# Q of two heads and two token tiles as seven block products in place of eight, in the second half of an attention kernel

## The chip, the cores and the metric

The kernel runs on one core of a Trainium2 chip. The metric is the device time of one execution in microseconds (us). The kernel before takes 1949.78 us (median of three runs, 1949.32 to 1949.82).

## The reference

```python
x = A_x                                   # 1 x 2048 x 640
xn = _layernorm(x, axis=-1)
# A: 32 heads of 128; of the cache only the last W = 512 keys are used
q = (xn @ wq)                             # 640 -> 32 x 128
scores = einsum(q, k) * 128 ** -0.5       # 2048 x 512 for each head
p = softmax(scores)
s = einsum(p, v) -> reshape(2048, 4096) @ wo   # back to 640
# B: dense block on the same xn
h = relu(xn @ w1 + b1) ** 2               # 640 -> 1728
g = silu(h @ w2 + b2)                     # 1728 -> 640
out = x + s * g
```

All arrays are float32.

## The kernel before, in words

Everything is held transposed: features on the 128 partitions, tokens along the free axis. The 2048 tokens are four tiles of 512 (0 to 3); the 640 features are five chunks of 128. Each operand of a matmul is split into two parts, `hi` (a copy by ACT, ScalarE, that rounds) and `lo` (what is left, by a subtraction on DVE, VectorE, or on POOL, GpSimd), and each product is three passes, hi x hi, hi x lo and lo x hi (`triple`). A pass is one matmul instruction with its weight load, 128x128 weights by 512 columns.

First come layernorm and the dense block for tiles 0 to 2 (its result g goes to DRAM as `g_d`; the normalised tiles, split, go there as `xT_d`). In that part tiles 1 and 2 (`T1`, `T2`) already get their 640 -> 1728 product by Winograd's form of Strassen's scheme: four blocks by four blocks in seven products (`t_sums`, `w_sums`, `prod`).

Then comes attention, in two halves: the first takes tiles 0 and 1, the second tiles 2 and 3. A half goes through 16 groups of two heads; a group has four units, one for each pair of a tile and a head. In a unit i, PE (TensorE) makes the scores `s` (four banks of PSUM, 12 matmuls), Q of a unit two later (`pq`, 5 chunks x 3 passes = 15 matmuls), `o` of the unit before (12), and the output products `r` of an earlier pair (15 on average; the sums over heads are kept in `acc`). That is 54 matmuls.

DVE takes the maxima of the four score banks (tile `rdm`), ACT gathers them (three small copies), DVE makes a row of them (`rowm`), which goes through DRAM by SP's queue (SyncE) and comes back broadcast as `bm`; DVE subtracts it from the scores (`e<-s,bm`, four times; this frees the score banks for the next unit). ACT takes the exponential and the hi part, POOL the lo part (`pt`) and the sum (`su`), DVE folds the sums (`rds`), gathered by ACT in the same way, and makes a reciprocal row (`sq`, `rows`), which comes back as `bs` and scales `o` on DVE. ACT and DVE then split `o` into `ot`. Q is split by ACT (`q_hi`) and DVE (`q_lo`). DVE also adds each `r` to `acc`.

What every engine does in which order is a plan: `at(when, f, ...)` puts a call at a time, the list is sorted by time, and every engine runs its own instructions in that order. The planner's times are only ranks; each instruction then waits for its data and for the buffers that it writes. PE's stream of instructions is also padded: `align(i, slot)` (L1411) calls `addr_align(BLOCK, ...)` with BLOCK = 256 before each of the four score products of a unit and once behind them, which puts no-operations (NOP) in until the next instruction's place is `FIRST_SLOT + 128 i + slot` modulo 256. `SLOTS` is (0, 11, 22, 33, 42). A unit thus has 128 places, and 86 of them lie between the last slot of one unit and the first of the next. A matmul takes two places, its weight load and itself.

In the second half tile 0's and 1's results are finished: the sums, x and g come from DRAM (`load_finish`), DVE multiplies (`fs<-fs,fg`), POOL adds, and SP stores; ten such pieces, one every four units. After the last units comes the dense block for tile 3 (`late_up`, tile `lu`; `late_down`, tile `ly`), which begins already in units 126 and 127, where no Q is left to make.

Of the kernel before, what the change touches and what calls it, by code (L numbers as in the profile page):

```python
# [14 lines left out]
P = 128  # L15
# [10 lines left out]
def kernel(  # L26
# [64 lines left out]
    s_d = [dpool.tile([P, DC, NT], F32, name=f"s_d{t}") for t in range(NTILE // 2)]  # L91
    h_d = {f: dpool.tile([P, NT], F32, name=f"h_d{f}") for f in range(FC - 4, FC)}
# [7 lines left out]
    T1, T2 = 1, 2  # L100
# [461 lines left out]
    def t_sums(q):  # L562
        e, o = 2 * q, 2 * q + 1
# [29 lines left out]
    def w_sums(p):  # L593
        a, b = WR[p, 0], WR[p, 1]
        a11, a12, a21, a22 = (w[:, k : 2 * NQ2 : 2, :] for w in (a, b) for k in range(2))
# [21 lines left out]
    def w_split(p, k):  # L617
# [10 lines left out]
        else:  # L628
            hi, lo = WB[p, "a2"] = wb("a2", [P, NQ2, P], f"wc{p}")
            pieces = [(hi, lo, b[:, 1 : 2 * NQ2 : 2, :])]  # L630
# [6 lines left out]
    def left(p, what, q):  # L637
        kind, at_ = {
            "a11": ("a1", (2 * q,)),
            "a12": ("a1", (2 * q + 1,)),  # L640
# [8 lines left out]
    def right(what, q):  # L649
        if what[0] == "t":  # L650
            return [w[:, q, :] for w in TS[int(what[1]) - 1]]
        k, j = int(what[1]) - 1, int(what[2])
        return [w[:, 2 * q + k, :] for w in XS[(T1, T2)[j - 1]]]
# [195 lines left out]
    def bank(name, k):  # L849
        return pools["psa"].tile([P, NT], F32, tag=f"qr{k}", name=name, bufs=1)  # L850
# [10 lines left out]

    def load_xT(hf, t, i, cs, queue=sp):
        queue.dma_start(raw(XT[hf, t][i])[:, cs, :], xT_d[hf * TPH + t][i][:, cs, :])

    def raw_tile(kind, name):
        n = D if kind in "qo" else W
        pool_of = pools["ep"] if kind in "qk" else ap
        return pool_of.tile([P, n], F32, tag=f"raw{kind}", name=name, bufs=1)
# [14 lines left out]

    def prep(kind, hf, h, eng=None):
        shape = {"q": [P, DC, DH], "k": [P, W], "v": [P, KC, DH], "o": [P, D]}[kind]
        home = {"q": WQ, "k": KT, "v": VV, "o": WO}[kind]
        hi, lo = home[hf, h] = pair(f"w{kind}", shape, f"w{kind}{hf}_{h}", 2 * G if kind == "o" else G)
        src = RAW.pop((kind, hf, h))
        act.activation(hi, src, AF.Copy)
        (eng or pool).tensor_tensor(lo, src, raw(hi), op=ALU.subtract)  # L890

    def q_mm(i, cs):
# [4 lines left out]
        for c in cs:  # L897
            triple(
                QPS[i],
                (ws[0][:, c, :], ws[1][:, c, :]),  # L900
# [3 lines left out]
            )  # L904

# [36 lines left out]
    def row(i, what):  # L942
# [13 lines left out]
        for args in BEHIND.pop((i, what), ()):  # L956
            load_xT(*args)
        bc = ap.tile([P, NT], F32, tag=f"b{what}", name=f"b{what}{i}", bufs=2)
# [12 lines left out]
    def p_hi(i, k):  # L971
        PT[i, k] = [
            ap.tile([P, 2, NT], F32R, tag=f"pt{n}", name=f"pt{i}_{k}_{n}", bufs=3)
# [21 lines left out]
    def v_mm(i, c):  # L995
        hf, g, t, h = units[i]
        if c == 0:
            if i % 2 or i < UPG:
# [53 lines left out]
    def load_finish(n, hf, t, d):  # L1052
        t0 = (hf * TPH + t) * NT
# [6 lines left out]
                "g": g_d[hf * TPH + t][:, d, :],  # L1060
# [7 lines left out]
    def finish(hf, t, d):  # L1068
        a = ACC[hf, t][:, d, :] if hf else FX.pop(("s", hf, t, d))
        (dve if hf else pool).tensor_tensor(a, a, FX.pop(("x", hf, t, d)), op=ALU.add)  # L1070
# [556 lines left out]
```

## Time and profile before

| | |
|---|---|
| median of three runs | 1949.78 us |
| span of the profiled execution | 1947.7 us, first to last instruction |
| PE, busy in the span | 1941.0 us, 8585 matmuls |
| DVE | 1599.4 us |
| ACT | 1242.3 us |
| POOL | 1348.4 us |
| DMA | 246.43 MB, mean 127 GB/s |
| units of attention | 128, from about 289 us on; the second half from about 1072 us on |

How to read it: busy time of an engine is the union of its instructions' times. In the timeline, a row merges equal neighbours of one engine: start, time from first start to last end, what, how many; brackets hold the idle time before it and what ended that. PE's matmuls overlap, so the distance of two starts is what counts there. The profiled execution is given by its span; what lies around the span is not listed for it, and the median of the runs stands 2.1 us above the span.

### The profile page before, as it was taken

The numbers are of one execution on the slowest core, as the hardware profiler recorded it, in microseconds if no ns is written. First come the engines' busy times: TensorE is split into PE (matmuls) and PEld (weight loads), VectorE is DVE, ScalarE is ACT, GpSimd is POOL, SyncE is SP. The second block draws the span as 40 slices with busy tenths as digits, with TensorE's granted clock in tenths as the row PEclk, the third lists the DMA queues.
The fourth block names the chain that finished last, engine by engine and source line by source line (L and its number), as shares of the span: only waits on it lengthen the run. The fifth ranks groups of instructions, "written<-read, shape, count | busy, mean of one in ns | idle before, by whom it ended". The sixth has DMA issues, their size and how long they took to land.

```text
span 1947.7 us, 28638 instructions
## 1 busy us (share of the span) xinstructions
PE 1941.0 (100%) x8585; PEld 1606.9 (83%) x8585; DVE 1599.4 (82%) x2760; ACT 1242.3 (64%) x2152; POOL 1348.4 (69%) x732
## 2 busy tenths in 40 slices
PE   9999999999999999999999999999999999999999
PEld 8888888888888888888888888888888888888887
DVE  6864747788888888888888878888888888888865
ACT  5665536766666666666666676666666666666643
POOL 1022107888888888888888878888888888888841
PEclk9999999999999999999999999999999999999999
DMA  6657953332222222222235433333333333323253
GB/s 207 198 195 252 367 190 114 95 93 91 91 90 92 93 91 91 92 92 92 92 100 183 140 109 109 114 114 114 114 114 114 113 115 113 98 92 92 84 189 119
DMA packets 147783, 246.43 MB, mean 127 GB/s; under 512 B 25188, under 2 KB 47478, under 8 KB 146358
## 3 DMA queue, kind: packets, MB, share of 16 engines
q1 hardware_dynamic: 144918, 232.65, 37.8%
q0 software_dynamic: 2576, 11.80, 1.5%
q8 instruction: 77, 1.26, 0.2%
q14 instruction: 68, 0.56, 0.1%
q10 hardware_dynamic: 144, 0.16, 0.0%
HBM read 213.59 MB, written 30.95 MB: 126 GB/s over the span
## 4 chain that ended last, share of the span: by engine, by line
PE 99%; DMA 0%; POOL 0%; DVE 0%; issue 0%; ACT 0%; SPq 0%; POOLq 0%
PE r L77 22%; PE pq L77 22%; PE o L77 18%; PE s L77 18%; PE py L77 7%; PE ph L77 3%; PE ly L77 2%; PE wa L77 2%; PE lu L77 2%; PE wy L77 1%; PE wx L77 1%; PE eu L77 1%; DMA xb<-in_x_dram 0%; PE px L77 0%; POOL xb L77 0%; DVE st L77 0%
## 5 line engine op out<-in xcount | busy, mean ns | idle before, releaser
L77 POOL TENSOR_TENSOR pt<-e,pt 128x1024 fp32r<-128x1024 f32 x256 | 614.8, 2402 | 113.3 <-ACT pt L77 62.3
L77 PE MATMUL r<-ot,wo 128*128 128x512 f32 x1920 | 496.6, 389 | 0.0
L77 PE MATMUL pq<-ax,wq 128*128 128x512 f32 x1920 | 456.0, 389 | 0.0
L77 PEld LDWEIGHTS r<-ot,wo 128*128 128x128 f32 x1920 | 360.4, 188 | 74.9
L77 PEld LDWEIGHTS pq<-ax,wq 128*128 128x128 f32 x1920 | 360.4, 188 | 74.8
L77 PE MATMUL o<-pt,wv 128*128 128x512 f32 x1536 | 369.2, 389 | 0.0
L77 PE MATMUL s<-q,wk 128*128 128x512 f32 x1536 | 369.0, 389 | 0.0
L77 DVE TRANSPOSE_TENSOR_REDUCE rdm<-s 128x16 f32<-128x512 f32 x512 | 348.3, 713 | 8.0 <-PE s L77 8.0
L77 ACT ACTIVATE e<-e 128x1024 f32<-128x1024 f32 x256 | 269.6, 1053 | 121.4 <-DVE e L77 74.3
L77 PEld LDWEIGHTS o<-pt,wv 128*128 128x128 f32 x1536 | 288.2, 188 | 60.2 <-POOL pt L77 0.4
L77 PEld LDWEIGHTS s<-q,wk 128*128 128x128 f32 x1536 | 288.3, 188 | 59.9
L77 DVE TENSOR_TENSOR e<-s,bm 128x512 f32<-128x512 f32 x512 | 311.9, 664 | 4.5 <-DMA bm<-m_d 4.1
L77 POOL TENSOR_TENSOR su<-e,e 128x1024 f32<-128x1024 f32 x128 | 308.7, 2412 | 0.0
L77 ACT ACTIVATE pt<-e 128x1024 fp32r<-128x1024 f32 x256 | 272.0, 1062 | 6.9
L77 ACT ACTIVATE rdm<-rdm 32x64 f32<-32x64 f32 x384 | 97.7, 254 | 184.6 <-DVE rdm L77 181.5
L77 DVE TENSOR_TENSOR acc<-r,acc 128x512 f32<-128x512 f32 x300 | 203.5, 678 | 13.2 <-PE r L77 13.1
L77 DVE TENSOR_TENSOR ot<-o,ot 128x512 fp32r<-128x512 f32 x128 | 88.5, 691 | 86.0 <-ACT ot L77 86.0
L77 DVE TRANSPOSE_TENSOR_REDUCE rds<-su 128x32 f32<-128x1024 f32 x128 | 158.3, 1236 | 0.2 <-POOL su L77 0.2
L77 ACT ACTIVATE q<-pq 128x512 fp32r<-128x512 f32 x128 | 76.6, 598 | 117.8 <-PE pq L77 117.8
L77 ACT ACTIVATE rds<-rds 32x32 f32<-32x32 f32 x384 | 89.5, 233 | 62.3 <-DVE rds L77 58.9
L77 POOL TENSOR_TENSOR wo<-or,wo 128x640 fp32r<-128x640 f32 x64 | 101.1, 1579 | 31.6 <-ACT wo L77 31.6
L77 POOL TENSOR_TENSOR wv<-vr,wv 128x512 fp32r<-128x512 f32 x64 | 83.2, 1300 | 54.1 <-ACT wv L77 54.1
(172 smaller groups left out, 2008.3 us busy)
## 6 DMA issues: line engine op xcount, KB each, us to landing
bm<-m_d SPq DMA_DIRECT2D x128, 256.0 KB
bs<-s_d SPq DMA_DIRECT2D x128, 256.0 KB
qr<-in_wq_dram SPq DMA_DIRECT2D x64, 320.0 KB
or<-in_wo_dram SPq DMA_DIRECT2D x64, 320.0 KB
kr<-in_kT_dram SPq DMA_DIRECT2D x64, 256.0 KB
vr<-in_v_dram SPq DMA_DIRECT2D x64, 256.0 KB
cw<-in_w_dram SPq DMA_DIRECT2D x26, 320.0 KB
h_m<-r SPq DMA_DIRECT2D x26, 256.0 KB
```

The source lines that it names most:

```text
L77: ins = method(*args, **kwargs)
```

## The change

The halves of attention take other tiles: the first tiles 0 and 3, the second tiles 1 and 2, for which the first part of the kernel already has the sums `T1` to `T4` of blocks of x. These go to DRAM (`TS_d`) by eight DMAs of POOL's queue. The blocks are now halves of the features (chunks 0, 1 and chunks 2, 3) and no longer the even and the odd chunks; the fifth chunk is done apart (`q_rest`).

In the first half, each group's two `wq` of the later use are turned into the sums S1 to S4 on DVE (`q_sums`, four additions of 128x256), split by ACT and POOL (`q_sum_hi`, `q_sum_lo`) and stored to DRAM with the plain blocks (`q_store`, nine calls a group). In the second half no `wq` is loaded or split; the ready pieces come from DRAM (`q_piece`, four a group) and the T blocks through a ring of three buffers (`q_ring`, six calls a group).

A group's Q in the second half is then, over the four units that begin two units ahead of it (slots 0 to 3):

- slot 0: product 5 in bank b, kept by ACT (`q_keep`, tile `qp5`); product 1 in bank a, copied by ACT to bank b (`q_seed`);
- slot 1: product 2 and a rest into b (Q of the first unit); product 6 into a; DVE adds `qp5` to a and puts it in b (`q_add`);
- slot 2: product 7 into a, kept by ACT (`qu3`); a rest and product 4 into a (Q of the second unit); DVE adds `qp5` to `qu3` and puts it in a (`q_add`);
- slot 3: product 3 and a rest into b (third unit); a rest into a (fourth unit).

The two banks that Q now holds were shared with `r` before. In the second half `r` has one bank (`psx`, tag x) and `o` has one. To make room, the buffers of `e` and `pt` go from three to two, that of `bs` from two to one. The times of `r` change with them (`R_AT_Q`), also in the last units. Only tile 0's five pieces are finished in the second half; tiles 1 and 2 are finished at the end (ten pieces), tile 3 in the late gate, for which its sums (`late_sum`) and its x tile (`load_late_x`) are loaded back.

How DVE's order moves, in unit 80 and the end of unit 79 (second half): the last maximum of unit 79 up to the first score to be shifted. Before:

```order
L77 TENSOR_REDUCE rdm79_13625<-s79_3_13636 128x16
L77 TENSOR_TENSOR acc1_1_12385<-r75_2_13551,acc1_1_12385 128x512
L77 TENSOR_REDUCE rowm79_13659<-rdm79_13625 32x16
L77 TENSOR_TENSOR o77_13578<-o77_13578,bs77_13576 128x512
L77 TENSOR_TENSOR ot77_13672<-o77_13578,ot77_13672 128x512
L77 TENSOR_REDUCE rds78_13681<-su78_13651 128x2x16
L77 SCALAR_TENSOR_TENSOR q81_1_13685<-pq81_13647,q81_0_13684 128x512
L77 TENSOR_TENSOR acc1_1_12385<-r75_4_13687,acc1_1_12385 128x512
L77 TENSOR_REDUCE sq2_2910<-rds78_13681 32x16
L77 RECIPROCAL sq2_2910<-sq2_2910 32x16
L77 STREAM_TRANSPOSE rows78_13707<-sq2_2910 32x32
L77 TENSOR_TENSOR e79_0_13729<-s79_0_13612,bm79_13663 128x512
```

The same place after:

```order
L77 TENSOR_REDUCE rdm79_14080<-s79_3_14091 128x16
L77 TENSOR_REDUCE rowm79_14119<-rdm79_14080 32x16
L77 TENSOR_TENSOR acc1_1_12867<-r75_3_14097,acc1_1_12867 128x512
L77 TENSOR_TENSOR o77_14031<-o77_14031,bs77_14029 128x512
L77 TENSOR_TENSOR ot77_14129<-o77_14031,ot77_14129 128x512
L77 TENSOR_REDUCE rds78_14141<-su78_14105 128x2x16
L77 SCALAR_TENSOR_TENSOR q80_1_14145<-pq20b_14006,q80_0_14144 128x512
L77 TENSOR_TENSOR pq20b_14166<-pq20a_13994,qp520_14001 128x512
L77 TENSOR_REDUCE sq2_2984<-rds78_14141 32x16
L77 RECIPROCAL sq2_2984<-sq2_2984 32x16
L77 STREAM_TRANSPOSE rows78_14172<-sq2_2984 32x32
L77 TENSOR_TENSOR acc1_1_12867<-r75_4_14151,acc1_1_12867 128x512
```

An `acc` that stood between the last maximum and the row made of the maxima now stands behind the row; the addition `pq20b` is new, and an `acc` stands ahead of the shift.

How ACT's order moves in unit 80 (slot 2 of group 20), from the gather of the maxima on. Before:

```order
L77 ACTIVATE rdm80_13763<-rdm80_13763 32x16x4 x3
L77 ACTIVATE pt79_1_0_13793<-e79_1_13735 128x1024
L77 ACTIVATE ot78_13808<-o78_13715 128x512
L77 ACTIVATE q82_0_13830<-pq82_13804 128x512
L77 ACTIVATE rds79_13817<-rds79_13817 32x16x2 x3
```

After:

```order
L77 ACTIVATE rdm80_14221<-rdm80_14221 32x16x4 x3
L77 ACTIVATE qu320_14250<-pq20a_13994 128x512
L77 ACTIVATE pt79_1_0_14252<-e79_1_14201 128x1024
L77 ACTIVATE ot78_14274<-o78_14180 128x512
L77 ACTIVATE q81_0_14297<-pq20a_13994 128x512
```

The copy `qu3` has come in ahead of `pt` and `ot`.

How PE's order moves in unit 126, the last but one: between the late block's first product `lu0` and `o125`. Before:

```order
L77 MATMUL lu0_20090<-ax1_1_1_11200,l1w0_0_19990 128x512
L77 MATMUL lu0_20090<-ax1_1_0_11199,l1w0_1_19991 128x512
L77 MATMUL r123_2_20112<-ot122_19820,wo1_28_0_19313 128x512 x2
L77 MATMUL r123_2_20112<-ot122_19820,wo1_28_1_19314 128x512
L77 MATMUL o125_20133<-pt125_0_0_20041,wv1_31_0_19986 128x512
```

After:

```order
L77 MATMUL lu0_20642<-ax2_0_0_20421,l1w0_20539 128x512
L77 MATMUL r123_1_20664<-ot122_20362,wo1_28_0_19845 128x512 x2
L77 MATMUL r123_1_20664<-ot122_20362,wo1_28_1_19846 128x512
L77 MATMUL r123_1_20664<-ot123_20505,wo1_29_0_19702 128x512 x2
L77 MATMUL r123_1_20664<-ot123_20505,wo1_29_1_19703 128x512
L77 MATMUL o125_20688<-pt125_0_0_20593,wv1_31_0_20535 128x512
```

Six matmuls of `r` stand there in place of three; ahead of `lu0` and behind `o125` there are six each, before and after. The unit has 57 matmuls in place of 54.

The core of the diff:

```diff
+    T1, T2 = 1, 2
+    TILE = ((0, LATE), (T1, T2))
+    TS_d = [dpool.tile([P, DC // 2, 2, NT], F32, name=f"ts_d{k}") for k in range(4)]
...
     def bank(name, k):
+        if k == "x":
+            return psx.tile([P, NT], F32, tag="x", name=name)
         return pools["psa"].tile([P, NT], F32, tag=f"qr{k}", name=name, bufs=1)
...
+    def q_piece(n, k):
+        w = QP[n, k] = wq_tile(f"qp{n}_{k}")
+        m = 4 if k in (0, 3) else DC
+        sp.dma_start(raw(w)[:, :, :m], wq_d[n % NG][k][:, :, :m])
...
+    def q_prod(n, k, b, blk, what, start=False):
+        w, ps = QP[n, k], QB[b]
+        for q in range(NQ2):
+            triple(ps, (w[:, 0, blk + q, :], w[:, 1, blk + q, :]), q_right(n, what, q), ...)
...
+    def q_keep(n, what, b):
+        QB[what] = raw_tile("q", f"q{what}{n}")[:, :NT]
+        act.activation(QB[what], QB[b], AF.Copy)
...
+    def q_seed(n):
+        q_bank(n, "b")
+        act.activation(QB["b"], QB["a"], AF.Copy)
+
+    def q_add(n, b, x):
+        src = QB[x]
+        q_bank(n, b)
+        dve.tensor_tensor(QB[b], src, QB["p5"], op=ALU.add)
...
-            E[i, k] = ap.tile([P, 2, NT], F32, tag="e", name=f"e{i}_{k}", bufs=3)
+            E[i, k] = ap.tile([P, 2, NT], F32, tag="e", name=f"e{i}_{k}", bufs=2)
...
-            if i % 2 or i < UPG:
+            if i % 2 or i < UPG or i >= NQS:
                 PO[i] = pools["psb"].tile([P, NT], F32, tag="o", name=f"o{i}", bufs=1)
...
+        for k in {1: (0,), 4: (1, 2), 5: (3,)}.get(p, ()):
+            for i in range(2):
+                pool.dma_start(TS_d[k][:, :, i, :], raw(TS[k][i]))
...
+    R_AT_Q = tuple(
+        tuple(((k * PERIOD + when, range(G)),) for k, when in places)
+        for places in (
+            ((3, 4.1), (3, 7.5), (4, 2.75), (4, 7.1), (4, 11.25)),
+            ((3, 2.75), (3, 7.1), (3, 11.25), (4, 2.75), (4, 7.75)),
+        )
+    )
...
+            if slot == 0:
+                on(4.1, q_first, n)
+                on(5.6, q_keep, n, "p5", "b")
+                on(5.5, q_second, n)
+                on(7.0, q_seed, n)
+            elif slot == 1:
+                on(4.1, q_prod, n, 1, "b", 0, "b21")
+                on(5.46, q_rest, n, 1, "b", 2, 0)
+                on(6.15, q_prod, n, 1, "a", 3, "t2")
+                on(8.45, q_add, n, "b", "a")
+            elif slot == 2:
+                on(2.75, q_prod, n, 2, "a", 3, "t3")
+                on(3.96, q_keep, n, "u3", "a")
+                on(5.5, q_rest, n, 2, "a", 2, 0)
+                on(6.18, q_prod, n, 2, "a", 0, "t4")
+                on(9.0, q_add, n, "a", "u3")
+            else:
+                on(4.1, q_prod, n, 3, "b", 2, "b22")
+                on(5.46, q_rest, n, 3, "b", 0, 1)
+                on(6.15, q_rest, n, 3, "a", 1, 1)
...
                 if i < NU - 1:
-                    for when, js in (R_AT_END if last else R_AT)[d]:
-                        on(when, r_mm, i, d, js, (R_BANK_END if last else R_BANK)[d])
+                    if last or i < NQS - 1:
+                        places, k = (R_AT_END, R_BANK_END) if last else (R_AT, R_BANK)
+                        k = k[d]
+                    else:
+                        places, k = R_AT_Q[t], "x"
+                    for when, js in places[d]:
+                        on(when, r_mm, i, d, js, k)
```

More of the change, by code (lines that the diff above doesn't have):

```diff
@@ L562, in t_sums @@
     def t_sums(q):
[L563 removed]
+        e, o = q, NQ2 + q
         (h1, l1), b12, b22 = XS[T1], XC.pop((T2, e)), XC.pop((T2, o))
@@ new lines, with q_right @@
+    RES = {
+        "b11": (0, 0),
+        "t1": (0, 2),
+        "b21": (1, 0),
+        "b22": (1, 2),
+    }
+    def q_right(n, what, q):
+        if (n, f"{what}{q}") in QR:
+            r = QR[n, f"{what}{q}"]
+            return r[:, 0, :], r[:, 1, :]
+        t, c = (1, 3) if what == "t4" else RES[what]
+        return [x[:, c + q, :] for x in XT[1, t]]
+    def q_prod(n, k, b, blk, what, start=False):
+        w, ps = QP[n, k], QB[b]
+        for q in range(NQ2):
+            triple(
+                ps,
+                (w[:, 0, blk + q, :], w[:, 1, blk + q, :]),
+                q_right(n, what, q),
+                start and q == 0,
+                q == NQ2 - 1,
+                skip_group_check=True,
+            )
@@ L1391 @@
             ):
-                if n or kind in "vo":
+                if (n or kind in "vo") and not (hf and kind == "q"):
                     at(base + when - 10.5, load_raw, kind, hf, h)
@@ L1398 @@
         at(u * PERIOD + 4.3, open_xT, 1, t)
-        pieces = [(1, t, i, slice(c, c + 1)) for c in range(DC) for i in range(2)]
+        pieces = [
+            (t, i, c) for c in ((2, 3, 0, 1, 4), (0, 1, 2, 3, 4))[t] for i in range(2)
+        ]
         places = [(u, "bm", 1 - t), (u - 1, "s", 2 - t), (u + 1, "m", 1), (u + 1, "bm", 1)]
```

223 lines of the change are left out of this document (185 added, 38 removed).

## The prediction

> **What bounds the kernel now.** I read the page's busy shares first, then the chain, then the second half alone by a window of 500 us, and then the timeline of one unit on DVE and PE.
>
> ```profile
> span 1947.7 us, 28638 instructions
> PE 1941.0 (100%) x8585; PEld 1606.9 (83%) x8585; DVE 1599.4 (82%) x2760; ACT 1242.3 (64%) x2152; POOL 1348.4 (69%) x732
> PE 99%; DMA 0%; POOL 0%; DVE 0%; issue 0%; ACT 0%; SPq 0%; POOLq 0%
> 1200.00:1700.00 500.00, 500.00 (x2206) 413.76 (x2205) 441.21 (x767) 328.50 (x571) 418.71 (x215) 1.00 0.36 112
> DVE ot L77 <- ACT ot L77: 27.3, 41, 0.7
> DVE rowm L77 <- ACT rdm L77: 21.1, 40, 0.9
> DVE sq L77 <- ACT rds L77: 4.5, 21, 0.2
> DVE acc L77 <- PE r L77: 1.8, 9, 0.2
> DVE e L77 <- DMA bm<-m_d: 1.1, 2, 0.9
> ```
>
> PE is the chain, at full granted clock (1.00), and never waits in the second half. The same 500 us read for DVE are the surprise: 441.2 us busy, 52.9 us of waits for ACT in the middle of its own sequences, and 2.9 us of waits for PE and DMA. DVE is busy or held by ACT's answers for 494 of 500 us. PE is the bound, but DVE stands right behind it, and the change takes work from the one and gives work to the other.
>
> To see how near, I take DVE apart. The first rows are the end of one unit, the others a whole one, and then PE's score products and ACT's copies:
>
> ```profile
> 1414.61 0.82 DVE L77 TENSOR_TENSOR fs<-fs,fg 128x512 f32<-128x512 f32 x1
> 1415.36 0.68 DVE L77 TENSOR_TENSOR acc<-r,acc 128x512 f32<-128x512 f32 x1
> 1415.96 2.49 DVE L77 TRANSPOSE_TENSOR_REDUCE rdm<-s 128x16 f32<-128x512 f32 x4
> 1419.30 0.41 DVE L77 TENSOR_REDUCE rowm<-rdm 32x16 f32<-32x256 f32 x1 [0.85 <-ACT rdm L77]
> 1419.64 0.67 DVE L77 TENSOR_TENSOR acc<-r,acc 128x512 f32<-128x512 f32 x1
> ...
> 1422.19 1.24 DVE L77 TRANSPOSE_TENSOR_REDUCE rds<-su 128x32 f32<-128x1024 f32 x1
> 1423.35 0.65 DVE L77 SCALAR_TENSOR_TENSOR q<-pq,q 128x512 fp32r<-128x512 f32 x1
> 1424.21 0.28 DVE L77 TENSOR_REDUCE sq<-rds 32x16 f32<-32x128 f32 x1 [0.21 <-ACT rds L77]
> ...
> 1424.93 2.43 DVE L77 TENSOR_TENSOR e<-s,bm 128x512 f32<-128x512 f32 x4
> 1427.29 0.67 DVE L77 TENSOR_TENSOR acc<-r,acc 128x512 f32<-128x512 f32 x1
> 1427.89 2.67 DVE L77 TRANSPOSE_TENSOR_REDUCE rdm<-s 128x16 f32<-128x512 f32 x4
> 1430.52 0.69 DVE L77 TENSOR_TENSOR acc<-r,acc 128x512 f32<-128x512 f32 x1
> 1431.41 0.41 DVE L77 TENSOR_REDUCE rowm<-rdm 32x16 f32<-32x256 f32 x1 [0.20 <-ACT rdm L77]
> 1431.75 0.68 DVE L77 TENSOR_TENSOR o<-o,bs 128x512 f32<-128x512 f32 x1
> 1433.09 0.69 DVE L77 TENSOR_TENSOR ot<-o,ot 128x512 fp32r<-128x512 f32 x1 [0.67 <-ACT ot L77]
> 1433.70 1.24 DVE L77 TRANSPOSE_TENSOR_REDUCE rds<-su 128x32 f32<-128x1024 f32 x1
> 1434.86 0.65 DVE L77 SCALAR_TENSOR_TENSOR q<-pq,q 128x512 fp32r<-128x512 f32 x1
> 1435.43 0.68 DVE L77 TENSOR_TENSOR acc<-r,acc 128x512 f32<-128x512 f32 x1
> 1436.03 0.25 DVE L77 TENSOR_REDUCE sq<-rds 32x16 f32<-32x128 f32 x1
> ...
> 1436.73 2.43 DVE L77 TENSOR_TENSOR e<-s,bm 128x512 f32<-128x512 f32 x4
> 1426.92 2.88 PE L77 MATMUL s<-q,wk 128*128 128x512 f32 x12
> 1429.64 0.84 PE L77 MATMUL r<-ot,wo 128*128 128x512 f32 x3
> 1406.93 1.06 ACT L77 ACTIVATE pt<-e 128x1024 fp32r<-128x1024 f32 x1
> 1409.44 0.60 ACT L77 ACTIVATE q<-pq 128x512 fp32r<-128x512 f32 x1 [0.86 <-PE pq L77]
> ```
>
> Read as distances of starts: four maxima and the wait for the gather, up to `rowm`, 3.34 (1415.96 to 1419.30; an `acc` in that gap, as at 1430.52, is free); `rowm` 0.34; `o` to `ot` 1.34, of which 0.67 is the wait for ACT; `ot` 0.61; `rds` 1.16; `q` 0.57; `acc` 0.60; `rds` to `sq` at least 2.02, since ACT's gather lies between; `sq` to the shift 0.70; the shift 2.36. One kind of unit then needs 3.34+0.34+0.60+1.34+0.61+2.02+0.70+2.36+0.60 = 11.91; the trace has 11.93 (1415.96 to 1427.89). The other kind, with an `acc` in the gap, needs 11.62. Four units need 47.1 of DVE, 47.8 where a finish (`fs`, 0.75) falls in. PE makes 12 matmuls in 2.72 (1426.92 to 1429.64), 0.2267 each; four units of 54 are 48.96. So PE leads by 1.1 to 1.9 us in four units, and no more.
>
> **The change part by part.**
>
> *PE's saving.* A group's Q was 4 x 15 = 60 matmuls. It is now seven products of 2 x 3 and four rests of 3: 54. Six less in 16 groups are 96 matmuls, 21.8 us if PE stays the bound: 210 x 0.2267 = 47.6 us in four units.
>
> *DVE in the second half.* It gets two additions a group. The nearest row is the same addition, PSUM and SBUF to PSUM, in the dense block:
>
> ```profile
> L77 DVE TENSOR_TENSOR wy<-wa,p 128x512 f32<-128x512 f32 x6 | 4.2, 700 | 9.3 <-ACT r L77 4.4 <-PE wa L77 4.1 <-ACT wa L77 0.8
> L77 PEldq NOP  x5: 13/13/13, 1841.7 to 1841.9; - x5
> L77 PEldq NOP  x11: 13/13/13, 0.8 to 1.6; - x11
> 1843.08 2.88 PE L77 MATMUL s<-q,wk 128*128 128x512 f32 x12
> ```
>
> It lasts 0.70; with the overlap that `acc` shows (0.67 long, 0.60 apart) I take 0.62. By the new order, from the first maximum of a unit to that of the next:
> - slot 0: 3.34+0.34+0.60+1.34+0.61+2.02+0.70+2.36+0.60 = 11.91 (one `acc` lies in the 2.02);
> - slot 1: 3.34+0.34+0.60+1.34+0.61+1.16+0.57+0.62+0.70+0.60+2.36 = 12.24;
> - slot 2: `qu3` (0.60) and `pt` (1.06) stand ahead of `ot` on ACT, so from `rowm` to DVE's `ot` it is the end of the gather, 0.55+1.05+0.60 and the handing over, 2.21; `o` and an `acc` fit in. 3.34+2.21+0.61+2.02+0.70+0.60+0.62+2.36 = 12.46;
> - slot 3 (two `q`): 3.34+0.34+0.60+1.34+0.61+1.16+0.57+0.57+0.60+0.70+2.36+0.60 = 12.79.
>
> That is 49.4 us a group, 2.3 more than before: 1.2 for the additions, and 1.2 because no `acc` lies in the gap ahead of `rowm` any more. It exceeds PE's 47.6 and also the 48.96 that a group takes now. The next scores wait for the shift to free their banks, so PE then waits 1.8 us a group for DVE: 16 x (49.4-48.96) = +7.0 us, in place of -21.8. Five groups still hold a finish of 0.75, which was under PE's cover and no longer is: +3.8. Half the finishes are gone to the end, where DVE has room (unpriced: 0.82 x 5 in the last 100 us). Bounds of this term: the sums may be 0.3 a group short either way (±5), and waits can only add.
>
> *Single banks, fewer buffers.* Lined up with these sums, `o` of slot 0 waits some 0.4 us for the one `o` bank, `o` of slot 3 some 0.3 for POOL's `pt`, the second half of slot 2's bank a up to 0.2 for `qu3`. Each lies on PE, which now has 1.8 us to spare in a group; between shift and maxima it may be 0.85 late without holding DVE. I take 0, upper bound 0.3 a group, 5 us.
>
> *DMA and SP.* A group loads four pieces of 512 or 640 KB and six blocks of 512, 5.4 MB, in place of two `wq` of 320 KB: 4.8 MB more in 49 us, about 97 GB/s on top of 112. SP issues all of them behind a `bm`, so the next row's trip through DRAM, and behind it DVE's shift, stands after them in the queue. The row above has 0.9 us as the longest wait for `bm`, twice in 41 units. I take 0; if each group's slot 1, where 1.6 MB stand ahead of the next row, met that wait once, 14 us. The removed `wq` copies and subtractions were on ACT and POOL, off the path.
>
> *First half.* Four DVE additions of half the size, 0.35 each by size from `acc`, raise 47.1 to 48.5 a group, under PE's 48.96; ACT's and POOL's splits and SP's nine stores stand behind the sums' row and have gaps. 0, upper bound 3 us if they are nearer to 0.4 and fall on a short unit. The eight DMAs of the T blocks on POOL and the late loads have no reader nearby: 0.
>
> *The pads.* In the steady units 39 or 42 matmuls follow the last slot, 84 of 86 places. In unit 126 there are now 45, 90 places and a wait: past the slot, so the pad runs to the next one modulo 256, 251 NOPs ahead of unit 127's scores. Counted this way the kernel before has a pad of 1 there. The rows above give the pace: five within 0.3 us, eleven in 0.8; 0.073 apart, though each lasts 13 ns. The first of a pad stands 1.4 us ahead of the scores it precedes (1841.7, 1843.08): so far runs PE's sequencer ahead. 251 x 0.073 = 18.3, less 1.4: +16.9 on PE with nothing beside it. By 13 ns each it would be 3.3-1.4 = +1.9; the pace is the nearer row, since it has NOPs one behind the other.
>
> [...]
>
> *Sum:* 1947.7+7.0+3.8+16.9 = 1975.4 in a profile; with the 2.1 us by which the median stands above the span, 1977.5.
>
> **The rivals.**
> - *PE stays the bound.* It needs DVE's group under 47.6, 1.8 below my sum: say that the gather's wait of 0.85 shrank in all four units to what it is with an `acc` inside. Nothing in the rows does that; the order puts nothing there. Then -21.8, and with the pad 1949.8-21.8+16.9 = 1944.9; without a costly pad 1930. This is the only way to faster.
> - *Short pads.* DVE bounds, but the 251 NOPs pass at 13 ns each (for: that duration; and tracing might itself space them). 1949.8+10.8+1.9 = 1962.5.
> - *Late `bm`.* All as forecast, and slot 1 waits 0.9 for the broadcast in each group: 1992.
> - *The seven products bring neither*: DVE's group comes out at 48.96 by chance and the pad is short: about 1951.
>
> **How the numbers follow.** My forecast (1970 to 1985 as its own range) 0.60; short pads 0.14; late `bm` or other stalls, 1985 and above, 0.13; PE bound with the pad 0.07, without 0.02; neither 0.04. 0.2% is 3.9 us, about what can be told from no change here: faster 0.09, same 0.05, slower 0.86. The range leaves out the PE-bound cases and the far end of the stalls: 1958 to 1992.
>
> **What would show it.** Right: 8489 matmuls; PE idle for DVE's `e` at the scores in the second half, about 1.8 us in four units; DVE without waits for PE there; groups 49.4 us apart; one gap of about 17 us on PE between unit 126's last `r` and unit 127's `s`, filled with NOPs. Wrong: groups 47.6 apart, or PE waiting for DMA or ACT, or no gap there.

## The result, and the profile after

The changed kernel takes 2264.95 us (median of four runs, 2256.5 to 2267.32), the kernel before 1949.55 (four runs): 1.161 times as long, 95% interval 1.159 to 1.163. The forecast was 1977.5 us, in a range of 1958 to 1992. The sign was right and the size was wrong by 287 us; what follows looks for where these came from.

The page of the changed kernel, its first two lines; then the same 500 us of the second half as before, by engine; then what ended the waits there (total us, times, longest):

```profile
span 2263.5 us, 29971 instructions
PE 2032.1 (90%) x8489; PEld 1623.0 (72%) x8489; DVE 1662.1 (73%) x2856; ACT 1257.9 (56%) x2232; POOL 1358.7 (60%) x772
```

```profile
1200.00:1700.00 500.00, 436.91 (x1793) 344.13 (x1793) 373.47 (x643) 279.00 (x499) 323.43 (x160) 0.96 0.57 175
```

```profile
PE s L77 <- DVE e L77: 39.8, 18, 4.6
DVE o L77 <- DMA bs<-s_d: 39.4, 19, 4.9
...
DVE e L77 <- DMA bm<-m_d: 24.6, 18, 3.1
...
PE o L77 <- DVE ot L77: 16.9, 9, 3.7
```

The 8489 matmuls are as counted. But PE is busy for 437 of 500 us where it was 500, and DVE for 373 where it was 441: no engine is the bound. DVE waits 64 us for the two broadcast rows `bs` and `bm`, where it waited 1.1 before, and PE waits for DVE. DMA went from 36% and 112 GB/s to 57% and 175 GB/s. The mean granted clock of PE fell from 1.000 to 0.961 over the whole span, so part of PE's busy time is slower matmuls behind its waits (the last section has the rows).

The times of the stages follow from the first matmul of a unit's scores in PE's timeline of the profiled execution:

| us | unit 0 begins at | unit 0 to 62 | 62 to 126 | 126 to 127 | 127 to the end | span |
|---|---|---|---|---|---|---|
| before | 289.7 | 757.5 | 783.6 | 12.2 | 104.6 | 1947.7 |
| after | 298.8 | 868.7 | 925.7 | 33.1 | 137.2 | 2263.5 |
| difference | +9.1 | +111.2 | +142.1 | +20.9 | +32.6 | +315.8 |

So every stage lost, the first half too, in which the change makes no product of its own. From unit 62 to 126 a group takes 57.9 us in the mean, for 49.0 before and the forecast 49.4. The stages follow one by one.

*The second half.* SP's waits from 1200 to 1700 us, first before, then after. SP sends a row to DRAM (`m_d`, `s_d`), waits until it has landed, and asks for its broadcast:

```profile
SPq L77 <- DMA m_d<-rowm: 48.8, 41, 2.5
SPq L77 <- DMA s_d<-rows: 43.3, 41, 2.0
```

```profile
SPq L77 <- DMA s_d<-rows: 151.7, 35, 7.0
SPq L77 <- DMA m_d<-rowm: 90.8, 34, 5.6
```

A row of sums was under way 1.1 us in the mean (43.3/41), and is 4.3 now; a row of maxima 1.2, and 2.7 now. SP's own timeline after shows what went ahead:

```profile
1529.67 0.33 SPq L77 DMA_DIRECT2D bm<-m_d  x1
1530.10 0.38 SPq L77 DMA_DIRECT2D qp<-wq_d  x1
1530.52 0.90 SPq L77 DMA_DIRECT2D tr_t<-ts_d  x2
1532.89 0.32 SPq L77 DMA_DIRECT2D s_d<-rows  x1
1539.18 0.32 SPq L77 DMA_DIRECT2D bs<-s_d  x1
```

A piece of `wq` and two T blocks, some 1.6 MB, are asked for from 1530.1 on; the 2 KB of `s_d` that follow at 1532.89 are back only at 1539.18. In between the DMA engines are nearly full, by stretches of PE's, PEld's, DVE's, ACT's and POOL's busy time, granted clock, DMA share and GB/s:

```profile
1532.00:1537.00 5.00, 4.81 (x22) 3.63 (x21) 3.70 (x8) 2.25 (x4) 1.29 (x1) 1.00 0.94 322
1537.00:1539.00 2.00, 2.00 (x10) 1.65 (x9) 2.00 (x5) 1.50 (x2) 1.32 (x1) 1.00 0.22 87
```

The row is back when they are free again.

*The first half.* Waits from 400 to 1000 us, and the four additions of the sums by form (count, busy us, mean ns; then idle before them):

```profile
PE s L77 <- DVE e L77: 45.4, 21, 3.4
DVE sw L77 <- POOL ss L77: 34.2, 10, 3.4
...
DVE e L77 <- DMA bm<-m_d: 11.7, 12, 1.4
```

```profile
L77 DVE TENSOR_TENSOR sw<-qr,qr 128x256 f32<-128x256 f32 x11 | 16.9, 1539 | 0.0
...
L77 DVE TENSOR_TENSOR sw<-qr,sw 128x256 f32<-128x256 f32 x11 | 15.4, 1402 | 0.0
...
L77 DVE TENSOR_TENSOR sw<-qr 128x256 f32<-128x256 f32 x10 | 4.3, 425 | 34.2 <-POOL ss L77 34.2
L77 DVE TENSOR_TENSOR sw<-sw,qr 128x256 f32<-128x256 f32 x10 | 4.2, 425 | 0.3
```

Two of the four last 1.5 and 1.4 us, the other two 0.43, with equal shapes: 3.8 us a group. The first of a group also waits 3.4 us for POOL, which splits the last sum of the group before out of the same buffer. All of it stands on DVE ahead of a shift: 7.2 us a group, in a stage whose group went from 48.9 to 56.0 in the mean.

*Units 126 and 127.* The row of the NOPs, and PE's timeline (the bracket is the idle time ahead of the row):

```profile
L77 PEldq NOP  x269: 13/13/13, 2107.8 to 2127.7; - x135
```

```profile
2109.59 1.52 PE L77 MATMUL r<-ot,wo 128*128 128x512 f32 x6
2126.35 4.66 PE L77 MATMUL s<-q,wk 128*128 128x512 f32 x12 [15.24 <-issue]
```

The pad is there, with PE idle for 15.2 us beside it.

*The end.* POOL's timeline, DVE's waits for the g of the finishes (from 2126 us on), and PE's wait that POOL ends:

```profile
2176.43 1.04 POOL L77 TENSOR_TENSOR lr<-lr 128x512 f32<-128x512 f32 x1
2188.93 1.64 POOL L77 TENSOR_TENSOR acc<-acc,fx 128x512 f32<-128x512 f32 x1 [11.46 <-DVE acc L77]
2190.53 2.11 POOL L77 TENSOR_TENSOR l1w<-l1r,l1w 128x640 fp32r<-128x640 f32 x1
```

```profile
DVE acc L77 <- DMA fg<-g_d: 34.9, 9, 6.4
```

```profile
2192.69 5.79 PE L77 MATMUL lu<-ax,l1w 128*128 128x512 f32 x13 [7.67 <-POOL l1w L77]
```

POOL stands 11.5 us at the addition of a finished piece, which waits for DVE's multiplication and that for its g from DRAM; the split of a late weight (`l1w`) stands behind it in POOL's order, and PE waits for that.

### The profile page after: what moved, and what is told of

Read it like the earlier page. It is cut to its first block, busy times and chain, and to the rows that moved or that the text cites. A ratio compares the mean times of both kernels' runs of the same rounds, so it can differ in the third digit from the quotient of the medians.

```text
span 2263.5 us, 29971 instructions
## 1 busy us (share of the span) xinstructions
PE 2032.1 (90%) x8489; PEld 1623.0 (72%) x8489; DVE 1662.1 (73%) x2856; ACT 1257.9 (56%) x2232; POOL 1358.7 (60%) x772
## 5 line engine op out<-in xcount | busy, mean ns | idle before, releaser
L77 PE MATMUL s<-q,wk 128*128 128x512 f32 x1536 | 423.9, 430 | 160.2 <-DVE e L77 144.9
L77 PEld LDWEIGHTS s<-q,wk 128*128 128x128 f32 x1536 | 313.7, 208 | 257.7 <-issue 105.5
L77 PE MATMUL o<-pt,wv 128*128 128x512 f32 x1536 | 389.9, 399 | 30.8 <-DVE ot L77 27.8
L77 DVE TRANSPOSE_TENSOR_REDUCE rdm<-s 128x16 f32<-128x512 f32 x512 | 328.6, 686 | 38.7 <-PE s L77 38.0
L77 PE MATMUL pq<-ax,wq 128*128 128x512 f32 x960 | 228.2, 389 | 0.0
L77 PEld LDWEIGHTS pq<-ax,wq 128*128 128x128 f32 x960 | 180.2, 188 | 37.7
L77 POOL TENSOR_TENSOR wo<-or,wo 128x640 fp32r<-128x640 f32 x64 | 107.3, 1676 | 81.8 <-ACT wo L77 81.8
L77 ACT ACTIVATE rds<-rds 32x32 f32<-32x32 f32 x384 | 90.0, 234 | 115.3 <-DVE rds L77 111.1
L77 ACT ACTIVATE ot<-o 128x512 fp32r<-128x512 f32 x128 | 76.5, 598 | 105.2 <-DVE o L77 105.1
L77 DVE TENSOR_TENSOR o<-o,bs 128x512 f32<-128x512 f32 x128 | 87.5, 684 | 63.9 <-DMA bs<-s_d 63.9
```

The costliest lines, as they stand in the source:

```text
L77: ins = method(*args, **kwargs)
```

## The experiments

"After" is the changed kernel; an edit is made to it, and its median is set against the 2264.95 us. The runs of after spread over 11 us and those of x6 over 14, so a few microseconds between two medians say nothing. The stage that an edit is aimed at was read from the run's own trace; the table behind the last run has them all.

**The pad.**

```diff
     def align(i, slot):
+        if i == NU - 1:
+            return
         pe.addr_align(BLOCK, ...)
```

> The four score products of unit 127 and the place behind them are no longer aligned, so no NOPs stand ahead of them; nothing else is changed. Theory (251 NOPs at 0.073 us each are the gap of 15.2 us on PE between unit 126 and unit 127): the gap falls under 2 us, unit 126 lasts 13 to 18 us in place of 33.0, and the kernel takes 2245 to 2250 us in place of 2265. Rival (the gap is something that PE's sequencer fetches or waits for, and the NOPs only stand in it): the gap stays above 10 us and the time within 4 us of 2265.

Measured: 2248.1 us, 16.9 less than after; unit 126 lasts 17.8 us. The NOPs were the gap. Of what is left over the 12.2 of before, 2.5 us are a wait for the late tile of x:

```profile
2103.33 3.14 PE L77 MATMUL lu<-ax,l1w 128*128 128x512 f32 x6 [2.46 <-DMA ax<-xT_d]
```

The twelve matmuls behind that wait (six of `lu`, six of `r`) take 4.9 us to the next start in place of 2.72, and three matmuls more than before another 0.7.

**The second half's loads, all of them, by another queue, at other times, and the T blocks alone.**

```diff
 def q_piece(n, k):                 # x2
+    (the two first pieces are kept and used for all groups)
 def q_ring(n, what):               # x2, x11
+    if n > NG or what in ("t30", "t31", "t40"):
+        QR[n, what] = QR[NG, what if what == "rest" else "t2" + what[2]]
+        return
-    sp.dma_start(...)              # x3: pieces and ring
+    act.dma_start(...)
-            at(t0 - PERIOD + 4.4, q_piece, n, slot)                     # x7
+            at(t0 - PERIOD + (4.4 if slot == 2 else 8.6), q_piece, n, slot)
```

In x7 the six calls of `q_ring` move in the same way: `t20` one unit earlier, `t21` and `t30` to 8.65 of the units before and of slot 0, `t31` and `t40` to 8.6 of slot 1, the rest to 8.65 of slot 2.

> In the second half the pieces of wq and the T blocks are loaded once, for the first group, and all later products use those; so the products of the later groups are of wrong data, with every matmul, addition and copy in place, and about 5.4 MB less is moved a group. Theory (rows on their way through DRAM stand behind these loads and come late): the waits for m_d fall from 2.6 to about 1.0 us each and those for s_d from 4.2 to about 1.0, DVE no longer waits for bm, a group of the second half takes 49.4 us or up to 51 in place of 57 to 58, and the kernel 2265 - 15.5 x 7 to 8 = 2141 to 2157 us. Rival (DVE's own sequence, lengthened by two additions and by waits for ACT and POOL, sets the group): groups stay above 55 us and the time above 2225.

> The same loads of pieces and T blocks, issued by ACT into its own DMA queue in place of SP's. Theory A (the small rows wait behind bulk loads of the same queue): trips of m_d and s_d fall to under 1.5 us, a group of the second half takes 50 to 52 us, the kernel 2160 to 2180 us; ACT has the room for ten issues of about 0.4 us a group. Theory B (the 16 DMA engines are shared by the queues and bulk on any queue delays the rows): trips stay at 3 us or more, and the time within 30 us of 2265.

> The same loads of pieces and T blocks on the same queue, at other times: two of them behind a bs, where 8 of the 12.4 of a unit's plan go by to the next row, and at most one behind a bm, where it is 4.4. Theory A (a row's trip is as long as the bytes that stand ahead of it in the DMA engines take, so it matters when they are issued): trips of m_d and s_d fall to 1.5 to 2.5 us, groups of the second half to 51 to 54 us, the kernel to 2165 to 2215. Rival B (the mean load on the DMA engines sets the trips, wherever the loads stand): groups stay above 56 us and the time within 25 of 2265.

> As the changed kernel, but only the loads of T blocks are left out after the first group (3.1 of the 5.4 MB a group); the pieces of wq are loaded as ever, so products use wrong T blocks. Theory (it is the bytes ahead of a row that make it late, so the loss falls faster than the bytes, once less than a unit's slack stands ahead): a group of the second half takes 50.5 to 52 us, the kernel 2155 to 2185. Rival (each extra load costs its share): groups of 53 to 55 us, the kernel 2200 to 2230.

Measured: without the loads (x2) 2149.5 us, 115.4 less than after; the second half takes 809.6 in place of 925.7 us, a group 50.4 (mean of units 64 to 124). By ACT's queue (x3) 2281.2, 16 more. At other times (x7) 2291.3, 26 more, just outside what the nearer of its two theories expected (25). Without the T blocks only (x11) 2161.7, 103.3 less, a group 50.9. SP's waits for the rows from 1200 to 1700 us, in x3 and in x11:

```profile
SPq L77 <- DMA m_d<-rowm: 113.3, 33, 5.8
SPq L77 <- DMA s_d<-rows: 82.6, 34, 7.2
```

```profile
SPq L77 <- DMA s_d<-rows: 68.7, 39, 4.1
SPq L77 <- DMA m_d<-rowm: 53.7, 39, 3.1
```

The loads are the cause, and not SP's queue: with the bulk in a queue of its own the rows still take 3.4 and 2.4 us, and DVE waits more for `bm` (65.4 us, where after has 24.6) and no longer for `bs`. The loads also stand at other times there, behind ACT's own instructions. The theory that it is the shared queue fell. Other times (x7) helped the row of sums: `bs` cost DVE 5.3 us in place of 39.4, `bm` still 21.0 for 24.6. But now the T blocks come late themselves:

```profile
PE pq23a L77 <- DMA tr_t<-ts_d: 3.7, 1, 3.7
```

One such wait, of 2.5 to 5.6 us, stands in slot 2 of each of the nine groups in this stretch, and in most of them PE also waits for a piece of `wq`, 1.8 to 7.2 us in all. So what the rows won in this layout the products lost. Leaving out 3.1 of 5.4 MB (57%) gives back 103.3 of 115.4 us (90%, x11). That speaks against a price per byte; since the T blocks also stand at other places than the pieces, amount and place are not told apart.

**The first half: sums, stores, sums on POOL, the last split earlier.**

```diff
 def q_sums(g, k):                  # x4; q_sum_hi and q_sum_lo likewise
+    return
 def q_store(g, k, lo, what):       # x5; loads then take wq_d[0]
+    if g:
+        return
-            dve.tensor_tensor(s1, a21, a22, op=ALU.add)                 # x6, all four
+            pool.tensor_tensor(s1, a21, a22, op=ALU.add)
-            u = k // 2 - 1 if end else k - 1                            # x12
+            u = k // 2 - 1 if end else min(k - 1, 1)
```

> In the first half the four additions of a group on DVE and the splits of their results on ACT and POOL are left out; the stores remain (of a tile of zeros), so the second half computes with zero sums. Theory (the additions on DVE cost 3.8 us a group because those with both sources in SBUF last 1.5 us and more beside POOL, and 3.1 us more by waiting for POOL's split of the group before): the first half from unit 0 to unit 62 takes 757 to 775 us in place of 868.7, and the kernel 2160 to 2172. Rival (the nine stores a group on SP's queue delay the row of maxima and with it DVE): the first half stays above 840 us, the kernel above 2235.

> The nine stores a group of the first half are made for group 0 alone, and the second half loads group 0's pieces each time; all additions and splits remain. Theory A (the stores have a price of their own, about the 30.6 us by which the first half without sums still stood above before: rows of maxima behind the stores): the first half from unit 0 to unit 62 falls from 868.7 to 835 to 845 us, the kernel to 2230 to 2240. Rival B (with the sums in place DVE is the later of the two, and the late rows hide beside it): the first half stays above 860 us, the kernel above 2255.

> The four additions of a group are made on POOL in place of DVE; all else stays. Theory (DVE is the first half's chain, and it loses 6.9 us a group to these additions: 3.8 in them, 3.1 in waits): the first half falls to what it was without sums, 785 to 800 us in place of 868.7, the kernel to 2182 to 2197. Rival (POOL, 76% busy there, becomes late with pt, which the o products and the sums of p wait for): the first half stays above 820 us.

> In the first half ACT's and POOL's split of the fourth sum stands one unit earlier, beside that of the third; nothing is left out. Theory (DVE's first addition of a group waits 3.1 us for that split, since the sums have one buffer, and this wait is on DVE's chain beside the 3.8 us of the additions): the wait goes, the additions stay slow, a group of the first half falls from 56 to 52.5 to 54 us, the first half from 868.7 to 820 to 840, the kernel to 2216 to 2236. Rival (DVE has slack there and the wait is filled by another): the first half stays above 860 us.

Measured: without the sums (x4) 2182.4 us, the first half 788.1 in place of 868.7; 757 to 775 were expected, so the sums are most of the loss and not all. Without the stores (x5) 2247.7 and 851.4, between what the two theories expected: the stores cost 17 us while the sums are there, and 29 without them (x4 to x9, below), so some of the late rows hide beside DVE's additions. (4.4 of the 29 are units 60 and 61, where the second half's loads begin.) From 400 to 1000 us DVE waits 38.9 us for `bm` in x4, and not at all in x9. With the sums on POOL (x6) 2190.6 and 796.3: POOL has the room, DVE had not. With the last split one unit earlier (x12) 2218.2 and 827.3: the wait for the single buffer alone was 41 us, some 2.7 a group.

**The end.**

```diff
 def load_finish(n, hf, t, d):
+    if hf and (t or d):
+        FX[n, hf, t, d] = FX[n, "one"]
+        return
     FX[n, hf, t, d] = tile = raw_tile(n, f"f{n}{hf}_{t}_{d}")
+    FX[n, "one"] = tile
```

> The ten pieces finished at the end use the x and the g that the first of them loaded (so nine of them get wrong data); 18 loads of 256 KB are left out, the multiplications, additions and stores stay. Theory (each finish waits on DVE for its g, since x and g have one buffer each; POOL's additions wait for that, and behind them stand the splits of the late weights that PE waits for): PE's waits for POOL's l1w, 14.1 us, and for ACT's l2w, 5.1 us, go, and with them the slower matmuls behind each; from unit 127's scores to the end 110 to 118 us in place of 137.2, the kernel 2245 to 2238. Rival (the late weights' own loads are late): the end keeps more than 130 us.

Measured: 2241.1 us; from unit 127 to the end 110.1 in place of 137.2. The finishes' loads are 27 of the 32.6 us that the end had lost.

**All of it out; then DVE's order; then one operand.**

```diff
+ (x1, x2, x4, x5 and x8 together, no TS_d)                                 # x9
-            ((3, 4.1), (3, 7.5), (4, 2.75), (4, 7.1), (4, 11.25)),         # x10: x9 and this
-            ((3, 2.75), (3, 7.1), (3, 11.25), (4, 2.75), (4, 7.75)),
+            ((3, 4.1), (3, 7.5), (4, 2.73), (4, 7.1), (4, 11.25)),
+            ((3, 2.73), (3, 7.1), (3, 11.25), (4, 2.73), (4, 7.75)),
-        src = QB[x]                                                        # x13: x10 and this
-        q_bank(n, b)
+        src = QB["a"]
+        if x != "u3":
+            q_bank(n, b)
         dve.tensor_tensor(QB[b], src, QB["p5"], op=ALU.add)
```

> All that the earlier runs named is left out together: the pad ahead of unit 127, the loads of pieces and T blocks after the first group, the sums and their splits, the stores after group 0, the second to tenth load of x and g at the end, and the eight DMAs of T blocks on POOL's queue (other tiles are loaded in their place). The data are wrong; every matmul of the change, ACT's copies to banks and DVE's two additions a group stay. If the named causes are the whole loss, each stage falls to before's, but for DVE's lengthened sequence in the second half: unit 0 begins at 290 us in place of 298.8, unit 0 to 62 takes 757 to 762 us, a group of the second half 50.3 as in the run without loads, unit 127's scores to the end 105 to 111, the kernel 1980 to 1992. If something else is lost: 2000 or more.

> As the kernel with all that left out, and with three of the r products of the second half ranked 0.02 earlier: PE's order stays the same to the row, but on DVE an acc stands again between the last maximum and the row of maxima, where DVE waits 0.85 us for ACT's gather, in three of four units. Theory (DVE's sequence sets the group: 0.60 of acc less what is left of the wait, 0.3 to 0.6 in each of three units): a group of the second half takes 48.5 to 49.4 us in place of 50.3, the kernel 13 to 28 us less than the one without this. Rival (the group above 49.4 is something else, PE's waits for Q's operands or for POOL): the time changes by less than 5 us.

> As the kernel with all left out and an acc in the gap, and with one operand changed: DVE's addition in slot 2 takes the bank it writes in place of the kept copy qu3 (so Q of two units is wrong); order, count and size stay. Theory (an addition with both sources in SBUF waits until POOL's instruction of that moment ends; with one source in PSUM it doesn't): the addition lasts 0.68 to 0.72 us in place of 1.27, slot 2 falls from 13.1 to 12.5, a group from 49.6 to 49.0 or 49.1, the kernel by 7 to 10 us to 1973 to 1976. Rival (the addition is long because it writes a bank that PE or ACT has just left, or by its place in the order): 1.27 stays, and the time within 3 us of 1983.

Measured: x9 1989.6 us (ratio 1.0204, 1.0189 to 1.0219), as expected and with each stage where it was expected: begin at 289.9, first half 759.3, end 111.1. The causes add up: 16.9 for the pad, 115.4 for the loads, 82.5 for the sums and 23.9 for the finishes by the single runs, 28.8 for the stores beside them (788.1 to 759.3) and 8.9 for the begin make 276.4; x9 is 275.3 under after. The last two are read from x9 itself; without them the four single runs make 238.7, of 237.6 that are left. Of the 40 us that x9 still stands above before, 25.6 are in the second half: 5.4 in its first group, which still loads and waits for rows (54.4 us), and 20.2 in the others, where DVE is the chain now. From 1200 to 1700 us DVE is busy for 432.8 us and waits 62.9 for ACT; PE waits 16.4 for its shift, about 1.7 a group. Some 12 us in unit 126 and at the end stay; 5.8 of them are PE's waits for the late x and for a weight's split on ACT, and the cause of the rest stays open. x10, 1983.2, takes 6.4 off, less than its 13 to 28: the `acc` is in the gap, but its `r` now ends up to 0.6 us too late for it. x13, 1973.1, takes another 10.2.

The addition of slot 2 and POOL's instruction of that moment, in x10 (DVE, then POOL):

```profile
1440.27 1.27 DVE L77 TENSOR_TENSOR pq23a<-qu,qp 128x512 f32<-128x512 f32 x1
```

```profile
1439.68 1.30 POOL L77 TENSOR_TENSOR wv<-vr,wv 128x512 fp32r<-128x512 f32 x1 [0.44 <-ACT wv L77]
1440.93 2.01 POOL L77 TENSOR_TENSOR wo<-or,wo 128x640 fp32r<-128x640 f32 x1
```

and in x13:

```profile
1436.17 0.68 DVE L77 TENSOR_TENSOR pq23a<-pq23a,qp 128x512 f32<-128x512 f32 x1
```

```profile
1435.58 1.30 POOL L77 TENSOR_TENSOR wv<-vr,wv 128x512 fp32r<-128x512 f32 x1 [0.42 <-ACT wv L77]
1436.84 1.56 POOL L77 TENSOR_TENSOR wo<-or,wo 128x640 fp32r<-128x640 f32 x1
```

In x10 POOL's `wv` ends at 1440.98, and DVE's addition, begun in the middle of it, 0.56 later at 1441.54; POOL's next instruction lasts 2.01 in place of 1.56. With one source in PSUM DVE's addition starts just so beside `wv`, and lasts 0.68. So I read these rows: with both sources in SBUF it waited for POOL's instruction to end (0.59 us more), and POOL's next for it (0.45 more). The long sums of the first half show the same, each ending 0.27 to 0.29 us behind a POOL instruction under way when it began; when a short one (0.43) begins, POOL mostly has none. Two were not held: in after the sums at 352.79 us, within 0.02 us of the start of POOL's `wo`, and at 353.12, still beside it, took 0.40 and 0.41 us, and `wo` 2.18 in place of 1.57.

**What can be mended with nothing left out.**

```diff
+ (x1, x6 and x12 together)
-        (pool if t == hf else dve).tensor_tensor(a, a, FX.pop(("x", hf, t, d)), op=ALU.add)
+        (dve if hf else pool).tensor_tensor(a, a, FX.pop(("x", hf, t, d)), op=ALU.add)
```

> The changed kernel with nothing left out and four edits: no pad ahead of unit 127, the sums of the first half on POOL, the fourth sum's split one unit earlier, and all ten additions of the finishes at the end on DVE. The loads of the second half stay as they are. By the earlier runs: the pad -17, the sums -75 to -80. The finishes' additions on DVE take the late weights' splits on POOL from behind the waits for g (-14 of PE's waits for them, and slower matmuls behind each), but DVE's splits of the second weights stay behind these waits: 137 to 122 to 132 us at the end. Sum 2150 to 2170 us. It would be no faster than before, since the second half's loads, 115 us, remain. If the waits at the end only move to DVE's own splits: the end keeps 137, and the kernel takes 2165 to 2175.

Measured: 2160.0 us (ratio 1.1083), the end 132.6. PE no longer waits for POOL's `l1w`, but for DVE's own split; DVE's order holds the waits for g, 34.4 us in all:

```profile
PE ly L77 <- DVE l2w L77: 14.6, 6, 4.2
```

So at the end it is the loads (x8) more than POOL: the wait goes with the engine that takes the finish. No version with all its work done came near the kernel before; x13, with all named losses out, is still 1.2% behind it.

The stages of all runs, with columns as in the table above; they are of the profiled execution, the median is of four runs:

| us | unit 0 begins at | unit 0 to 62 | 62 to 126 | 126 to 127 | 127 to the end | median |
|---|---|---|---|---|---|---|
| x1 no pad | 300.4 | 870.9 | 923.2 | 17.8 | 135.9 | 2248.1 |
| x2 no loads | 298.4 | 868.5 | 809.6 | 33.2 | 137.1 | 2149.5 |
| x3 ACT's queue | 298.3 | 869.2 | 940.9 | 33.0 | 137.9 | 2281.2 |
| x4 no sums | 296.3 | 788.1 | 924.7 | 34.1 | 138.3 | 2182.4 |
| x5 no stores | 298.3 | 851.4 | 922.0 | 33.2 | 139.7 | 2247.7 |
| x6 sums on POOL | 300.2 | 796.3 | 926.1 | 34.6 | 138.3 | 2190.6 |
| x7 spread | 298.4 | 868.1 | 942.3 | 33.3 | 137.9 | 2291.3 |
| x8 one finish load | 298.4 | 870.4 | 925.9 | 33.3 | 110.1 | 2241.1 |
| x9 all out | 289.9 | 759.3 | 809.2 | 18.0 | 111.1 | 1989.6 |
| x10 acc in gap | 289.8 | 761.8 | 801.1 | 18.4 | 112.2 | 1983.2 |
| x11 no T blocks | 297.8 | 872.1 | 818.2 | 33.9 | 138.4 | 2161.7 |
| x12 split earlier | 299.6 | 827.3 | 920.0 | 31.4 | 137.1 | 2218.2 |
| x13 add from PSUM | 290.0 | 760.7 | 792.8 | 18.2 | 109.5 | 1973.1 |
| x14 mended | 297.6 | 790.3 | 917.8 | 18.0 | 132.6 | 2160.0 |

## Why the prediction was wrong

- *PE's saving*: 96 matmuls less is right, and that it brings nothing too, since PE is not the bound. The reason, DVE's sequence, is what x9 shows: PE's 1.7 us a group of waits for the shift there, for the forecast 1.8. In the changed kernel itself late rows hid that.
- *DVE's sequence in the second half*, forecast at 49.4 us a group. With everything else out, x9's DVE timeline gives it: the first maxima of the units of slots 3, 0, 1 and 2, the slot 2 addition, the shift behind it, and the next maxima.

```profile
1394.09 2.50 DVE L77 TRANSPOSE_TENSOR_REDUCE rdm<-s 128x16 f32<-128x512 f32 x4
...
1406.91 2.49 DVE L77 TRANSPOSE_TENSOR_REDUCE rdm<-s 128x16 f32<-128x512 f32 x4
...
1418.91 2.49 DVE L77 TRANSPOSE_TENSOR_REDUCE rdm<-s 128x16 f32<-128x512 f32 x4
...
1431.91 2.49 DVE L77 TRANSPOSE_TENSOR_REDUCE rdm<-s 128x16 f32<-128x512 f32 x4
...
1441.44 1.27 DVE L77 TENSOR_TENSOR pq23a<-qu,qp 128x512 f32<-128x512 f32 x1
1442.63 2.47 DVE L77 TENSOR_TENSOR e<-s,bm 128x512 f32<-128x512 f32 x4
1445.03 2.50 DVE L77 TRANSPOSE_TENSOR_REDUCE rdm<-s 128x16 f32<-128x512 f32 x4
```

  That is 12.82 for slot 3, then 12.00, 12.40 (13.00 less a finish of 0.60) and 13.12, for 12.79, 11.91, 12.24 and 12.46. In all 50.3. The mis-sized term is slot 2's addition: priced 0.62 by a row with one source in PSUM, it takes 1.19 to the next start, with both in SBUF. And the reading of the gap was half right: an `acc` back in it is worth 0.5 a group (x10), not 1.2. This stage lost 25.6 us in x9, 20.2 without the first group, which still loads, for the forecast 10.8.
- *Single banks, fewer buffers*: 0, at most 0.3 a group. The bound held: in x2 the weight loads of `o` wait some 0.4 us a group for POOL's `pt` and 0.2 for DVE, PE itself 0.3 for the copy `qu3`.
- *DMA and SP*: the step that failed. 0 was taken and 14 us set as the bound, from the longest wait for `bm` in a trace that had 112 GB/s; it is 115. That row tells what the old load did to a row and nothing of the new. What was needed was in the trace of before: its fullest stretch.

```profile
200.00:250.00 50.00, 50.00 (x222) 41.42 (x221) 35.91 (x54) 27.50 (x45) 8.15 (x15) 1.00 0.96 358
```

  At 358 GB/s, with the DMA engines 96% busy, the 1.6 MB that the prediction itself put ahead of the next row take some 4.6 us, an estimate from that row; the rows of sums took 4.3 us in the mean. It named this rival, late `bm`, and priced it by the old trace, 0.9 us once a group; and it left the other row out: `bs` has 39.4 of the 64.0 us that DVE waited for both.
- *First half*: 0 and at most 3 us; it is 111, of which the sums are 81 (x4) and the stores 29 (x4 to x9). Four things were missed in one sentence there: the additions were scaled by size from `acc`, which has a source in PSUM; the one buffer of the sums makes DVE wait for POOL (41 us, x12); the splits "have gaps", but POOL's gaps come too late for that; and stores are bytes ahead of a row as loads are (29 us, x4 to x9).
- *T blocks and late loads*: 0, "no reader nearby". x9 begins 8.9 us earlier than after; in after, PE waits there for ACT, 4.8 us in all from 60 to 290 us, where before and x9 have no wait of PE's, and ACT waits for a store of `h` to land. Of x9's edits only the T blocks' stores stand ahead of unit 0, so the loss is theirs; that it comes by the queueing of stores is argued from the trace:

```profile
194.99 1.65 PE L77 MATMUL py<-ch,cw 128*128 128x512 f32 x3 [2.52 <-ACT r L77]
```

```profile
194.25 0.69 ACT L77 ACTIVATE r<-wy,b_sb 128x512 f32<-128x512 f32 x1 [3.65 <-DMA h_m<-r]
```

  And the late x does have a reader, `lu` in unit 126.
- *Finishes at the end*: "DVE has room". It has, but the ten pieces have one buffer each for x and g, and DVE's waits for g (34.9 us) hold what stands behind them in its order and in POOL's: 24 us (x8).
- *The pad*: +16.9 forecast, 16.9 measured (x1). That NOPs pass at the pace of 0.073 us was right (269 in 19.9 us, the row of units 126 and 127, are 0.074 each); that the two numbers are the same is partly luck. The gap itself is 15.2 us; another 1.8 are the score products behind it, 4.50 us to the next start (2130.85) for 2.72, which the prediction did not have. The rival of short pads is out.

Pad and DVE's term, the two that had a price, were forecast at 28 us, of the 315 that the change cost. Of the miss of 287 us some 9 are the size of DVE's term; nearly all the rest is in terms set to zero.

## What to carry to other kernels

Here 1.6 MB put ahead of a row of 2 KB, on which DVE's chain depends, take some 4.6 us by the 358 GB/s of the fullest stretch of before (an estimate), and the rows of sums took 4.3 us in the mean, for 1.1 before; ACT's queue in place of SP's did not help (2281.2 us for 2264.95). So work out that time against the slack of the small transfer for each place, not the mean load. Take the price of an elementwise instruction from a row with its kind of operands: with both sources in SBUF beside a busy POOL slot 2's addition took 1.27 us (x10), with one in PSUM 0.68 (x13). Every term that is set to zero needs the row that covers it, and a look at what the same engine's queue holds behind each new wait.

## What the runs showed of the hardware that was not expected

- DVE's additions with both sources in SBUF lasted longer where a POOL instruction was under way: 1.54 and 1.40 us in the mean for 128x256 (after, 400 to 1000 us), for 0.43 where mostly none was; for 128x512 1.27 (x10), for 0.68 with one source in PSUM (x13), and POOL's next instruction 2.01 in place of 1.56.
- NOPs on PE stood 0.074 us apart (after, 269 from 2107.8 to 2127.7 us) though each lasted 13 ns; the pad of 251 left PE idle for 15.2 us.
- Behind the pad PE's matmuls were slower for a while: 12 score products took 4.66 us behind the gap of 15.2 us (the row shown with the pad) and 2.88 in the steady stream before the change, so the gap cost 1.8 us more than its length. The granted clock (third number from the end) was 0.50 there, 1.00 again from 2131 to 2135 us, and 0.50 also behind a wait of 2.4 us for the late x. Behind waits of 0.35 and 1.36 us in after (score products at 1416.17 and 1332.02 us) it was 1.00, and the 12 products took 3.03 and 2.96 us. The rows of after:

```profile
2104.00:2106.00 2.00, 2.00 (x6) 1.61 (x6) 0.00 (x0) 0.72 (x2) 0.00 (x0) 0.50 0.30 71
2126.00:2128.00 2.00, 1.65 (x4) 1.39 (x5) 0.00 (x0) 0.00 (x0) 0.00 (x0) 0.50 0.00 0
2131.00:2135.00 4.00, 4.00 (x20) 3.29 (x19) 2.48 (x6) 2.42 (x5) 1.19 (x1) 1.00 0.01 1
```
